# Hourglass attention and a gated MLP on one core: a replanned start and q, k loads in three pieces

## Chip, core and metric

The kernel runs on one core of one Trainium2 chip. Its engines are TensorE (PE), ScalarE (ACT), VectorE (DVE), GpSimd (POOL) and SyncE (SP, which only issues DMAs here). The metric is the device time of one execution in microseconds (us), the median of several.

## What is computed

q, k, v have the shape 8 x 8 x 576 x 64 (batch, head, position, value). The attention has two parts that are added: one over means of four neighbouring positions (144 of them), spread back over the four, and a local one in which each position sees only those less than four away.

```python
q_d = q.reshape(B, H, Sd, factor, D).mean(axis=3)      # k_d, v_d alike
out_d = sm_attn(q_d, k_d, v_d)
out_up = np.repeat(out_d, factor, axis=2)
mask = np.abs(pos[:, None] - pos[None, :]) < factor
scores = np.where(mask, scale * np.matmul(q, k.transpose(0, 1, 3, 2)), -1000000000.0)
out_local = np.matmul(softmax(scores), v)
attn = out_up + out_local                              # -> x, 4608 x 512
h = x @ w_in                                           # 512 x 2048
g = h * (1.0 / (1.0 + np.exp(-h)))
return g @ w_out                                       # 2048 x 512
```

## The kernel before

**Work.** The 64 heads are handled as 32 pairs of heads; pairs 4b to 4b+3 are batch b, and batch b gives 576 of the 4608 rows of x. For each pair p the jobs are:

- loads of q and k (into tile qkb as bf16, cast by the DMA that POOL issues; pair 0 comes in float32 into qk and is cast by DVE and ACT) and of v (four jobs lv p h j on SP, 64 x 5 rows of 64 values each, cast by POOL in job cv);
- T: 36 transposes of 64 x 64 on PE (line 810), then the evictions eq and ek from PSUM into qT and kT (line 565), and two sums over four positions on DVE (line 845);
- S: scores (20 + 4 + 8 matmuls with the mask's bias for the first eight pairs), then two exponentials on ACT (line 893);
- Z: sums of the exponentials (12 matmuls), on DVE turned into factors (lines 964, 968, 974);
- VP: means of v (9 matmuls) for the first eight pairs, evicted as vd;
- PV: 28 matmuls, then m on DVE (line 990) and a on POOL (line 1018), which writes the pair's part of xT.

G1 is x times w_in, 9 blocks of 512 rows with 16 groups of 4 matmuls each; a group is followed by a tanh on ACT (line 1043) and a product on DVE (line 1047). G2 is the product with w_out, 4 x 4 parts of 4 matmuls per block. The first block of G1 needs batch 0 only, the second needs batches 0 and 1. All matmuls but the transposes are recorded under line 571, the helper mm.

**Order.** Nothing of the order is written out. The class Plan simulates the jobs in Python while the kernel is built: each job has costs, jobs that it waits for, buffers and PSUM banks that it takes, and a due time; each engine, when it comes free, takes the ready job with the smallest due time. The order that results on each engine is what the program holds, so each engine and each issuing queue runs strictly in that order. For PE the function pick prefers jobs of kind A (those of pairs 0 to 7), then visits V of later pairs, then G1 and G2. D(p, left) gives the due times: 22 + 1.5 (p - 3) - left for pairs 0 to 3, and 42 + 3 (p - 7) - left for pairs 4 to 7. For T left is 8.5, for S 6.5, for Z 4.5, for VP 4.0 and for PV 2.4.

Four things in Plan.run matter here:

- PE jobs that start before COLD[0] us are taken to last COLD[1] times as long.
- Before WARM_END, when the planner sees PE idle ahead of a job, it puts filler matmuls in front of it (jb.fill): products of the constant tile dz into a free PSUM bank, whose results nobody reads.
- code and FETCH stand for the loading of PE's instructions: a job with mm matmuls takes 2 mm instructions, and after each 256 of them PE waits until FETCH us after the last such wait (5.2 before 110 us, then 4.5). But the constructor of Job sets mm to 0 after it has taken the keywords, so that no job has a count and the model is never used.
- The weights are issued by POOL as w0 to w7 (four pieces of w_in, four of w_out), each behind a gate, W_GATE: w0 after pair 2's last v load has landed, w1 to w4 after that of pairs 4 to 7, w5 to w7 after the issue of k of pairs 8 to 10. load_order holds back the loads of pairs 4 to 7 in the plan until pair 3's last v load is issued, and those of pair 8 until w2 has landed.

```python
n = int((now - max(busy["PE"], self.freed[b]) - WARM_GAP) / 0.43 if now < WARM_COLD else
        (now - max(busy["PE"], self.freed[b]) - WARM_GAP) * WARM_PART / 0.22)
if n > 0:
    j.fill = (n, b)
```

The planner reaches each engine's queue: what it moves on PE moves with its evictions on ACT and DVE, its a jobs on POOL and its loads on POOL and SP.

Of the kernel before, what the change touches and what calls it, by code (L numbers as in the profile page):

```python
# [6 lines left out]
AF = mybir.ActivationFunctionType  # L7
# [3 lines left out]
BF16 = mybir.dt.bfloat16  # L11
# [5 lines left out]
NPAIR = B_ * H_ // 2  # L17
NSUP = 9
XR = 2048
COLD = (8.0, 1.65)  # L20
WARM_END, WARM_GAP, WARM_PART, WARM_COLD = 115.0, 0.4, 0.6, 7.0
FETCH = (5.2, 110.0, 4.5)
ALONE = 0.8
TW = 8
N_QK, N_VS, N_VQ, N_QKB, N_VB, N_VD, N_T, N_P, N_ZR, N_RB, N_XO = 1, 4, 2, 6, 5, 5, 3, 4, 2, 2, 3
GS_PE = 0
VP_PE = 8

SPLIT = 8
# [5 lines left out]
LEAD = 6  # L35
K_ENG = "DVE"
FRESH = 2.2


CV_ENG = "POOL"  # L40
# [10 lines left out]


def E_ENG(p, x):
    return ("ACT", "DVE") if p < 8 else "ACT"


def G_ENG(p, x):
    return ("DVE", "ACT")


def G1_BANKS(j):
# [26 lines left out]
def HOLD(p):  # L88
    return ["S3"] if p == 4 else []
# [148 lines left out]
class Job:  # L238
# [3 lines left out]
    def __init__(self, name, eng, cost, emit, **kw):  # L242
        self.name, self.emit = name, emit
        self.eng = (eng,) if isinstance(eng, str) else eng
        self.cost = cost if isinstance(cost, dict) else {e: cost for e in self.eng}
        self.pre, self.take, self.use, self.bank, self.marks = (), (), (), None, {}
        self.due, self.work, self.port, self.kind, self.thr, self.gran = 0.0, 0.0, False, None, None, 0.093
        for k, v in kw.items():
            setattr(self, k, v)
        self.ran, self.last, self.succ, self.end, self.mm, self.fill = None, None, [], None, 0, None  # L250


class Plan:
# [241 lines left out]
def bass_hourglass_attn__then__act_silu_kernel(  # L495
# [9 lines left out]
    with kctx:  # L505
# [25 lines left out]
        vs = sb("vs", [128, 10, 64], F32, N_VS)  # L531
        vq = sb("vq", [128, 4, 256], F32, N_VQ)
        vt = sb("vt", [128, 4, 128], F32)
        qkb = sb("qkb", [128, 2, 576], BF16, N_QKB)
        vb = sb("vb", [128, 10, 64], BF16, N_VB)
        vd = sb("vd", [128, 4, 64], BF16, N_VD)
        qT = sb("qT", [128, S_], BF16, N_T)
# [133 lines left out]
        def rows(t, p, n, off):  # L671
            return bass.AP(tensor=t.tensor, offset=t.offset + (128 * p + off) * 576, ap=[[576, n], [1, 576]])

        def dma(name, eng, out_, in_, r, w, sem, work, cost, hold=(), **kw):
            def emit(j):
                P.op(j.ran, lambda s: s.dma_start(out_(), in_()), r() if r else [], w(), sem(), after=gates(hold))  # L676
            kw["pre"] = list(kw.get("pre", ())) + list(hold)
            J(name, eng, cost, emit, work=work, **kw)

        def loads(p, order):  # L680
            if p == 0:
                dma("lkx", LD_ENG("kx", 0), lambda: kx[64:128, :], lambda: rows(k, 0, 64, 0), None, lambda: rkx, lambda: "kx",
                    0.45, 0.43, due=order["kx"], take=[("qkb", -1)])
            for x, (t, n, off) in enumerate(((q, 128, 0), (k, 128 if p < NPAIR - 1 else 64, 64))):
                if p in SW:
                    dma(f"c{'qk'[x]}{p}", "POOL", lambda x=x, n=n: qkb[S("qkb", p)][0:n, x, :],
                        lambda t=t, n=n, off=off: rows(t, p, n, off), None, lambda x=x: [R(f"qkb{S('qkb', p)}{x}")],
                        lambda x=x: f"qkb{S('qkb', p)}{x}", 0.87, 0.57, gran=0.106, take=[("qkb", p)], due=-60 + p if p < 4 else D(p, 26.0),
                        hold=order.get(("gate", p), ()))
                    continue  # L690
                dma(f"l{'qk'[x]}{p}", LD_ENG("qk"[x], p), lambda x=x, n=n: qk[S("qk", p)][0:n, x, :],
                    lambda t=t, n=n, off=off: rows(t, p, n, off), None, lambda x=x: [R(f"qk{S('qk', p)}{x}")],
                    lambda x=x: f"qk{S('qk', p)}{x}", 0.85 * n / 128, 0.43, take=[("qk", p)] + ([("qkb", 0)] if p == 0 else []), due=order["qk", p],
                    hold=order.get(("gate", p), ()))
            for h in range(2):
                for j in range(2):
                    def emit(jb, h=h, j=j):
                        s = S("vs", p)
                        sem, w = f"vs{s}{h}{j}", [R(f"vs{s}{h}{j}")]
                        base = v[(2 * p + h) // H_, (2 * p + h) % H_]  # L700
                        T_, o = base.tensor, base.offset + (288 * j - 3) * D_
                        d, lo, hi = vs[s][half(j), 5 * h:5 * h + 5, :], 0, 5
                        if (p, h, j) == (0, 0, 0):
                            lo = 1
                            P.op(jb.ran, lambda e: e.dma_start(vs[s][3:64, 0, :], bass.AP(
                                tensor=T_, offset=base.offset, ap=[[64, 61], [1, 64]])), [], w, sem, after=gates(["vz"] + list(order.get(("gate", p), ()))))
                        if (p, h, j) == (NPAIR - 1, 1, 1):
                            hi = 4
                            P.op(jb.ran, lambda e: e.dma_start(vs[s][64:123, 9, :], bass.AP(
                                tensor=T_, offset=base.offset + 517 * D_, ap=[[64, 59], [1, 64]])), [], w, sem)  # L710
                        P.op(jb.ran, lambda e: e.dma_start(d[:, lo:hi, :], bass.AP(
                            tensor=T_, offset=o + 58 * 64 * lo, ap=[[64, 64], [58 * 64, hi - lo], [1, 64]])), [], w, sem,
                            after=gates(order.get(("gate", p), ())))
                    J(f"lv{p}{h}{j}", LD_ENG("v", p), 0.64, emit, work=0.39, gran=0.018, take=[("vs", p)],
                      due=order["v", p], pre=list(order.get(("gate", p), ())) + (["vz"] if p == 0 else []))
            if p >= VP_PE:
                def emit(jb):
                    i = S("vq", p)
                    base = v[2 * p // H_, 2 * p % H_]
                    T_, o = base.tensor, base.offset  # L720
                    P.op("SP", lambda e: e.dma_start(vq[i][:, 0:4:2, :], bass.AP(
                        tensor=T_, offset=o, ap=[[256, 128], [S_ * D_, 2], [1, 256]])), [], [R(f"vqm{i}")], f"vq{i}")
                    for j in range(2):
                        P.op("SP", lambda e, j=j: e.dma_start(vq[i][64 * j:64 * j + 16, 1:4:2, :], bass.AP(
                            tensor=T_, offset=o + 128 * 256, ap=[[256, 16], [S_ * D_, 2], [1, 256]])),
                            [R(f"vqc{i}1"), R(f"vqc{i}3")], [R(f"vqe{i}{j}")], f"vqe{i}{j}")
                J(f"lvq{p}", "SP", 1.6, emit, work=0.85, gran=0.046, take=[("vq", p)], due=order["vq", p],
                  pre=list(order.get(("gate", p), ())) + [f"vqz{(p - VP_PE) % N_VQ}"])
# [18 lines left out]
        def casts(p):  # L747
# [2 lines left out]

            def one(x):
                def emit(jb):
                    P.op(jb.ran, lambda e, a=i(), b=j(): copy(jb.ran, e, qkb[b][:, x, :], qk[a][:, x, :]),
                         [R(f"qk{i()}{x}")], [R(f"qkb{j()}{x}")])
                return emit

            if p == 0:
                def emit(jb):
                    P.op("ACT", lambda e, b=S("qkb", -1): e.activation(qkb[b][64:128, 1, :], kx[64:128, :], AF.Copy),
                         rkx, [R(f"qkb{S('qkb', -1)}1")])  # L760
                J("ckx", "ACT", 0.65, emit, pre=["lkx"], take=[("qkb", -1)], due=D(0, 9.4))
            use = dict(take=[("qkb", p)], use=[("qk", p)])
            if p in SW:
                pass
            elif p < CAST2:
                for x in range(2):
                    eng = C_ENG[p][x]
                    J(f"c{'qk'[x]}{p}", eng, {"DVE": 0.5, "ACT": 0.65, "POOL": 0.6}, one(x), pre=[f"l{'qk'[x]}{p}"],
                      port=True, due=D(p, 9.3), **use)
            else:  # L770
                def emit(jb):
                    P.op("POOL", lambda e, a=i(), b=j(): e.tensor_copy(qkb[b][:, :, :], qk[a][:, :, :]),
                         [R(f"qk{i()}0"), R(f"qk{i()}1")], [R(f"qkb{j()}0"), R(f"qkb{j()}1")])
                J(f"cq{p}", "POOL", 1.15, emit, pre=[f"lq{p}", f"lk{p}"] + HOLD(p), port=True, due=D(p, 10.3), marks={f"ck{p}": 1.0}, **use)

            def emitv(jb):
                a, b = S("vs", p), S("vb", p)
# [24 lines left out]
        def pe_T(p):  # L802
            a, b = S("qkb", p), S("qkb", p - 1)
            tiles = ((0, 0, 0, a), (0, 1, 1, a), (1, 1, 0, a), (1, 0, 1, b))
            for r in range(9):
                for j, h, x, n in tiles:
                    t, c = t_home(p, x, r)
                    o = PS[half(h), t, c:c + 32].bitcast(BF16)
                    w = qkb[n][half(j), x, 64 * r:64 * r + 64]
                    P.op("PE", lambda e, o=o, w=w, j=j: e.transpose(o, w, idn[half(j), :]),  # L810
                         [R("idn"), R(f"qkb{n}{x}")], [rB[t]])

# [6 lines left out]

        def after_T(p):  # L820
            keys = dict(take=[("T", p)])
            grp = p < GS_PE

            def evict(x):
                def emit(jb):
# [471 lines left out]
```

## Time and profile before

| | us |
|---|---|
| median of 3 runs | 341.86 (341.33 to 343.66) |
| the profiled execution | 342.31 |
| its span, first to last instruction | 340.5 |
| PE busy in the span | 326.8 |
| mean clock granted to TensorE | 0.970 of full |
| first matmul of G1 | 36.32 after the span's start |
| first matmul of G2 | 73.05 |

All times inside the profile count from the span's start. A busy share of PE is not a share of its peak: matmuls overlap in the array, and their ends are modelled. In a row of the timeline the bracket at the end gives the idle time of the engine before it and what ended it; "issue" there means that nothing the profile shows was waited for. A DMA share is the mean over the core's 16 DMA engines; it can pass 1. Queue 0 holds the DMAs that POOL issues, queue 1 those of SP, queue 10 those of ACT, queue 8 code.

### The profile page before, as it was taken

What the parts mean: (1) busy time and instruction counts of PE and PEld (TensorE: products, weight loads), DVE (VectorE), ACT (ScalarE), POOL (GpSimd) and SP (SyncE); (2) the same over time, 40 slices, a digit from 0 to 9 for tenths busy, and PEclk for the clock granted to TensorE, in tenths of its full rate; (3) what the DMA queues carried; (4) which work ended last, traced back from release to release, by engine and by line L of the source; (5) the groups of instructions that cost most, each with busy time, mean ns of one, the idle gap of its engine ahead of it and who ended that gap; (6) DMA issues with size and microseconds to landing.
All of it is one profiled execution on the core that took longest, in us unless ns stands there. A gap on an engine that the chain in (4) does not pass through costs nothing.

```text
span 340.5 us, 10780 instructions
## 1 busy us (share of the span) xinstructions
PE 326.8 (96%) x4623; PEld 213.9 (63%) x4623; DVE 229.6 (67%) x410; ACT 179.0 (53%) x317; POOL 156.6 (46%) x211
## 2 busy tenths in 40 slices
PE   5587999999999999999999999999999999999996
PEld 2465677865555775587557755785577558866544
DVE  6586989866667885788577857796767556754200
ACT  5542756665544765476447645664656416644221
POOL 7363498435679667970698068704400140000000
PEclk9755999999999999999999999999999999999999
DMA  8997879999878976996398339500100010000112
GB/s 168 175 252 156 255 181 212 198 229 234 172 178 195 213 177 151 209 202 174 76 240 180 81 57 249 115 1 33 66 31 2 33 64 31 2 1 31 62 64 92
DMA packets 70666, 44.59 MB, mean 131 GB/s; under 512 B 45914, under 2 KB 63770, under 8 KB 70618
## 3 DMA queue, kind: packets, MB, share of 16 engines
q1 hardware_dynamic: 56378, 28.00, 30.8%
q0 software_dynamic: 13088, 15.36, 26.2%
q8 instruction: 36, 0.59, 0.7%
q10 hardware_dynamic: 1152, 0.54, 0.7%
q14 instruction: 12, 0.10, 0.1%
HBM read 45.61 MB, written 9.44 MB: 162 GB/s over the span
## 4 chain that ended last, share of the span: by engine, by line
PE 92%; DMA 2%; DVE 2%; issue 2%; POOL 1%; ACT 0%; POOLq 0%
PE PS L571 89%; PE PS L810 3%; DMA qkb<-in_k_dram 2%; DVE Pt L899 1%; POOL qkb L676 0%; DVE qd L845 0%; POOL gT L601 0%; DVE Rb L974 0%; DVE qT L565 0%; DVE kd L845 0%; DVE zt L964 0%; DVE zr L968 0%; ACT osb L1076 0%; DVE vd L565 0%; POOL idw L610 0%
## 5 line engine op out<-in xcount | busy, mean ns | idle before, releaser
L571 PE MATMUL PS<-xT,w_in_sb 128*128 128x512 f32 x576 | 141.2, 399 | 0.0
L571 PE MATMUL PS<-w_out_bf,gT 128*128 128x512 bf16 (+1 forms) x592 | 131.3, 374 | 0.0
L571 PEld LDWEIGHTS PS<-xT,w_in_sb 128*128 128x128 f32 x576 | 106.7, 188 | 24.7 <-DVE gT L1047 0.7
L1047 DVE SCALAR_TENSOR_TENSOR gT<-th,PS 128x512 bf16<-128x512 f32 x144 | 96.9, 683 | 37.0 <-ACT th L1043 36.3
L1043 ACT ACTIVATE th<-PS 128x512 f32<-128x512 f32 x144 | 86.1, 599 | 54.2 <-PE PS L571 46.0
L571 PEld LDWEIGHTS PS<-w_out_bf,gT 128*128 128x128 bf16 x592 | 54.7, 98 | 62.9 <-issue 3.5
L1018 POOL TENSOR_TENSOR xT<-xo 128x576 fp32r<-128x576 f32 (+5 forms) x48 | 43.5, 919 | 51.5 <-DVE xo L990 51.4
L565 POOL CAST vb<-vs 128x640 bf16<-128x640 f32 x32 | 24.4, 767 | 57.3 <-PE PS L571 42.5
L1100 ACT ACTIVATE osb<-PS 128x512 f32<-128x512 f32 x35 | 21.1, 603 | 53.6 <-PE PS L571 53.6
L893 ACT ACTIVATE Pt<-PS 128x576 bf16<-128x576 f32 x32 | 20.8, 649 | 33.0 <-PE PS L571 32.8
L785 POOL TENSOR_TENSOR vt<-vq 128x512 f32<-128x512 f32 x24 | 30.8, 1285 | 10.0 <-DMA vq<-in_v_dram 9.9
L990 DVE TENSOR_TENSOR xo<-PS,Rb 128x720 f32<-128x720 f32 x32 | 28.6, 893 | 5.1 <-PE PS L571 4.9
L974 DVE STREAM_TRANSPOSE Rb<-zr 128x768 f32<-128x768 f32 x32 | 30.9, 964 | 0.1
L899 DVE TENSOR_TENSOR Pt<-Pt,mask 128x576 bf16<-128x576 bf16 x24 | 16.3, 677 | 20.9 <-ACT Pt L893 20.9
L565 ACT ACTIVATE qT<-PS 128x576 bf16<-128x576 bf16 x30 | 19.8, 659 | 9.4 <-PE PS L810 9.4
L810 PE MATMUL PS<-idn,qkb 64*64 64x64 bf16 x1152 | 17.5, 201 | 7.5 <-issue 3.9
L845 DVE TENSOR_REDUCE qd<-qT 128x144 bf16<-128x576 bf16 x32 | 22.9, 716 | 1.5 <-ACT qT L565 1.4
L845 DVE TENSOR_REDUCE kd<-kT 128x144 bf16<-128x576 bf16 x32 | 23.0, 718 | 0.0
L964 DVE STREAM_TRANSPOSE zt<-PS 128x96 f32<-128x96 f32 x32 | 8.8, 274 | 20.2 <-PE PS L571 20.2
L565 ACT ACTIVATE kT<-PS 128x576 bf16<-128x576 bf16 x30 | 20.0, 665 | 1.6 <-PE PS L810 1.6
L810 PEld LDWEIGHTS PS<-idn,qkb 64*64 64x64 bf16 x1152 | 14.2, 115 | 9.5 <-issue 4.5
L676 POOL DMA_DIRECT2D qkb<-in_k_dram x31 | 17.1, 553 | 5.1 <-PE PS L810 5.1
(56 smaller groups left out, 229.3 us busy)
## 6 DMA issues: line engine op xcount, KB each, us to landing
vs<-in_v_dram SPq DMA_DIRECT2D x123, 80.0 KB, 4.6
out_dram<-osb SPq DMA_DIRECT2D x35, 256.0 KB, 3.6
vq<-in_v_dram SPq DMA_DIRECT2D x24, 256.0 KB, 4.3
qkb<-in_q_dram POOLq DMA_DIRECT2D x31, 144.0 KB, 5.0
qkb<-in_k_dram POOLq DMA_DIRECT2D x30, 144.0 KB, 5.4
w_in_sb<-in_moe_w_in_dram POOLq DMA_DIRECT2D x4, 1024.0 KB, 7.4
w_out_bf<-in_moe_w_out_dram POOLq DMA_DIRECT2D x4, 512.0 KB, 14.3
vq<-in_v_dram SPq DMA_DIRECT2D x48, 32.0 KB, 3.9
```

The lines of the kernel that those rows point to most:

```text
L565: return e.activation(out_, in_, AF.Copy) if eng == "ACT" else e.tensor_copy(out_, in_)
L571: P.op("PE", lambda t: t.matmul(out_, lhsT, rhs, start=start, stop=stop, skip_group_check=True), r, w)
L785: P.op("POOL", lambda g: g.tensor_tensor(vt[:, :, :], vq[n][:, :, 0:128], vq[n][:, :, 128:256], ALU.add), [R(f"vqm{n}"), R(f"vqe{n}0"), R( ...
L810: P.op("PE", lambda e, o=o, w=w, j=j: e.transpose(o, w, idn[half(j), :]), [R("idn"), R(f"qkb{n}{x}")], [rB[t]])
L845: P.op("DVE", lambda e: e.tensor_reduce(dst, src.rearrange("p (g r) -> p g r", r=4), AX.X, ALU.add), [R(f"{'qk'[x]}T{s}")], [R(f"{'qk'[x]} ...
L893: P.op("ACT", lambda e: e.activation(d[:, :, :], PS[:, b[0]:b[1] + 1, a:e_], AF.Exp, scale=sc), [rB[b[0]], rB[b[1]]], [R(f"P{m}" if local ...
L974: P.op("DVE", lambda e: e.transpose(Rb[n][:, :].rearrange("p (c q) -> p c q", q=32), zr[z][:, :].unsqueeze(2).to_broadcast([128, 24, 32])) ...
L990: P.op("DVE", lambda e: e.tensor_tensor(xo[x][:, :, :], PS[:, bb[0]:bb[1] + 1, 0:360], Rb[u][:, :].rearrange("p (x c) -> p x c", x=2)[:, : ...
L1018: P.op("POOL", lambda g, dst=dst, in0=in0, in1=in1: g.tensor_tensor(dst, in0, in1, ALU.add), [R(f"xo{x}")], xblk(kc, t + a, t + e_))
L1043: P.op("ACT", lambda e: e.activation(th[x][:, :], PS[:, b, :], AF.Tanh, scale=0.5), [rB[b]], [R(f"th{x}")])
L1047: P.op("DVE", lambda e: e.scalar_tensor_tensor(gT[j % 2][:, f, :], th[x][:, :], 1.0, PS[:, b, :], ALU.add, ALU.mult), [rB[b], R(f"th{x}")] ...
L1100: P.op("ACT", lambda e, s=S("osb", n), b=bank(key)[0]: e.activation(osb[s][:, :], PS[:, b, :], AF.Copy, scale=0.5), [rB[bank(key)[0]]], [R ...
```

## The change

Every edit is in the start of the kernel or in the planner:

- the model of code loading comes into use, since mm is no longer reset; PE jobs count 1.5 times their cost until 34 us of the plan, not 1.65 times until 8 us;
- WARM_END is 0, so no fillers are put in (the memset of dz stays);
- the evictions of T of pairs 5 to 7 may go to ACT only, those of pairs 0 to 4 to ACT or DVE as before;
- a row of q or k (576 values) is loaded in three pieces of 192, each to its own 200-value stretch of qkb; the transposes and the casts of pair 0 follow that layout;
- a branch in casts that no pair took is left out, and GS_PE and G_ENG are written in another form with the same effect here.

By the planner's new costs, jobs of pairs 0 to 3 come ahead of those of pairs 4 to 7 where both are ready.

```diff
-COLD = (8.0, 1.65)
-WARM_END, WARM_GAP, WARM_PART, WARM_COLD = 115.0, 0.4, 0.6, 7.0
+COLD = (34.0, 1.5)
+WARM_END, WARM_GAP, WARM_PART, WARM_COLD = 0.0, 0.4, 0.6, 7.0
...
-GS_PE = 0
+GS_PE = ()
...
+AD = ("ACT", "DVE")
+E_EARLY = (AD, AD, AD, AD, AD, "ACT", "ACT", "ACT")
...
 def E_ENG(p, x):
-    return ("ACT", "DVE") if p < 8 else "ACT"
+    return E_EARLY[p] if p < 8 else "ACT"
...
+        self.mm = 0
         for k, v in kw.items():
             setattr(self, k, v)
-        self.ran, self.last, self.succ, self.end, self.mm, self.fill = None, None, [], None, 0, None
+        self.ran, self.last, self.succ, self.end, self.fill = None, None, [], None, None
...
-        qkb = sb("qkb", [128, 2, 576], BF16, N_QKB)
+        qkb = sb("qkb", [128, 2, 3, 200], BF16, N_QKB)
...
+        def rows_3(t, p, n, off):
+            return bass.AP(tensor=t.tensor, offset=t.offset + (128 * p + off) * 576, ap=[[576, n], [192, 3], [1, 192]])
+
+        def parts(x):
+            return x.rearrange("p (a b) -> p a b", a=3)
...
-                    dma(f"c{'qk'[x]}{p}", "POOL", lambda x=x, n=n: qkb[S("qkb", p)][0:n, x, :],
-                        lambda t=t, n=n, off=off: rows(t, p, n, off), None, lambda x=x: [R(f"qkb{S('qkb', p)}{x}")],
+                    dma(f"c{'qk'[x]}{p}", "POOL", lambda x=x, n=n: qkb[S("qkb", p)][0:n, x, :, 0:192],
+                        lambda t=t, n=n, off=off: rows_3(t, p, n, off), None, lambda x=x: [R(f"qkb{S('qkb', p)}{x}")],
...
-                    w = qkb[n][half(j), x, 64 * r:64 * r + 64]
+                    w = qkb[n][half(j), x, r // 3, 64 * (r % 3):64 * (r % 3) + 64]
...
-            grp = p < GS_PE
+            grp = p in GS_PE
```

More of the change, by code (lines that the diff above doesn't have):

```diff
@@ L37 @@
 FRESH = 2.2
+AD = ("ACT", "DVE")
+E_EARLY = (AD, AD, AD, AD, AD, "ACT", "ACT", "ACT")
+G_EVICT = ("DVE", "ACT")
 CV_ENG = "POOL"
@@ L53, in E_ENG @@
 def E_ENG(p, x):
-    return ("ACT", "DVE") if p < 8 else "ACT"
+    return E_EARLY[p] if p < 8 else "ACT"
 def G_ENG(p, x):
-    return ("DVE", "ACT")
+    return G_EVICT
 def G1_BANKS(j):
@@ L752, in emit @@
                 def emit(jb):
-                    P.op(jb.ran, lambda e, a=i(), b=j(): copy(jb.ran, e, qkb[b][:, x, :], qk[a][:, x, :]),
+                    P.op(jb.ran, lambda e, a=i(), b=j(): copy(jb.ran, e, qkb[b][:, x, :, 0:192], parts(qk[a][:, x, :])),
                          [R(f"qk{i()}{x}")], [R(f"qkb{j()}{x}")])
@@ L758, in emit @@
                 def emit(jb):
-                    P.op("ACT", lambda e, b=S("qkb", -1): e.activation(qkb[b][64:128, 1, :], kx[64:128, :], AF.Copy),
+                    P.op("ACT", lambda e, b=S("qkb", -1): e.activation(qkb[b][64:128, 1, :, 0:192], parts(kx[64:128, :]), AF.Copy),
                          rkx, [R(f"qkb{S('qkb', -1)}1")])
@@ L769, in casts @@
                       port=True, due=D(p, 9.3), **use)
[L770 to L774, printed above, removed]
             def emitv(jb):
```

## The prediction

> **What bounds the kernel now.** I read the page first, then busy time by stretch, then TensorE's timeline of the first 45 us, then the times at which loads landed.
>
> From the page: each engine's busy share, the slices, the queues.
>
> ```profile
> PE 326.8 (96%) x4623; PEld 213.9 (63%) x4623; DVE 229.6 (67%) x410; ACT 179.0 (53%) x317; POOL 156.6 (46%) x211
> ...
> PE   5587999999999999999999999999999999999996
> ...
> PEclk9755999999999999999999999999999999999999
> ...
> q1 hardware_dynamic: 56378, 28.00, 30.8%
> q0 software_dynamic: 13088, 15.36, 26.2%
> q8 instruction: 36, 0.59, 0.7%
> ```
>
> PE is full from the fifth slice on. What can be won lies in the first 36 us, where the clock is also half. The 36 packets of queue 8 load code: 0.59 MB in 36 pieces is 16 KB each, and 4623 matmuls and as many weight loads over 36 are 257, so one piece holds about 256 of PE's instructions, that is 128 matmuls.
>
> Busy time by stretch (first two columns: stretch and length; then busy time, with counts, of PE, PEld, DVE, ACT, POOL; granted clock; DMA share; GB/s):
>
> ```profile
> 12.00:16.00 4.00, 2.56 (x104) 1.83 (x93) 1.41 (x2) 3.15 (x6) 2.06 (x4) 0.69 0.86 159
> 20.00:24.00 4.00, 2.88 (x95) 2.33 (x90) 3.86 (x9) 1.55 (x4) 2.83 (x4) 0.50 1.20 314
> 24.00:28.00 4.00, 2.48 (x67) 1.78 (x64) 1.69 (x3) 0.72 (x3) 0.90 (x1) 0.50 1.22 213
> 28.00:32.00 4.00, 3.60 (x83) 2.35 (x82) 2.54 (x5) 1.58 (x3) 1.51 (x2) 0.50 0.73 159
> 32.00:36.00 4.00, 4.00 (x132) 2.30 (x132) 4.00 (x9) 2.27 (x4) 2.40 (x3) 0.63 0.38 86
> 36.00:40.00 4.00, 4.00 (x100) 3.07 (x92) 4.00 (x8) 3.16 (x7) 1.67 (x3) 1.00 1.01 278
> ```
>
> The clock is 0.50 to 32 us and 1.00 from 36. The clock's own records put the rise at 34.93, after 17.07 us at half. PE is not idle after 28.4.
>
> PE's timeline (start, length, what, count, idle time before it and its releaser):
>
> ```profile
> 16.56 0.22 PE L810 MATMUL PS<-idn,qkb 64*64 64x64 bf16 x4 [2.00 <-issue]
> ...
> 21.94 0.27 PE L571 MATMUL PS<-qT,kT 64*64 64x58 bf16 x5 [1.12 <-issue]
> ...
> 28.40 0.43 PE L810 MATMUL PS<-idn,qkb 64*64 64x64 bf16 x16 [1.92 <-issue]
> ...
> 29.35 0.61 PE L571 MATMUL PS<-dz 128*128 128x512 bf16 x1
> ...
> 31.32 0.47 PE L571 MATMUL PS<-Pt,vb 64*64 64x58 bf16 x20
> ...
> 33.90 1.31 PE L571 MATMUL PS<-dz 128*128 128x512 bf16 x3
> ...
> 36.32 2.11 PE L571 MATMUL PS<-xT,w_in_sb 128*128 128x512 f32 x8
> ```
>
> The three waits on nothing ("issue", 5.04 us) fall 128 matmuls apart: they are waits for code. PE ran out again 5.38 and 6.46 us after it resumed, whatever it had to do. So to 28.4 us PE is paced by code, and fillers (dz) and early transposes of pairs 4 and 5 spend that code. The product with w_in (G1) begins at 36.32; pair 3's PV, the last it needs, began at 31.32.
>
> **The change part by part.** Times are against the profiled execution: 342.31 us, a span of 340.5 and 1.8 around it. That is 0.45 above the median, 341.86.
>
> *Fillers gone.* There are 23. The six from 29.35 on stand in a stretch without idle time. From each row's start to the next: 0.40 (29.35 to 29.75), 0.54, 0.54, and 1.24 for the three at 33.90, in all 2.72 us. Freed time at half clock is worth half, and the clock rises when it rises: up to 33.90 the work slides by 1.48; the 1.18 us from 35.14 to 36.32 at full clock then take 2.36 at half from 32.42 and end at 34.8. So G1 could follow at 34.8, not 36.32: **-1.5**. Ends: 0 and -2.7. The 13 fillers from 1.46 on and those at 9.7 ran while PE waited for q and k: removing them frees nothing there.
>
> *Code spent on fillers.* 17 fillers ran before 28.4: 34 of 256 instructions, at 5.9 us a piece (mean of 5.38 and 6.46): **-0.8**, ends 0 and -0.9.
>
> *Batch 0 first.* The planner now keeps the matmul counts that it used to reset to 0, so it sees code waits, and it takes 1.5 times as long for PE jobs until 34 us. Batch-0 jobs have the earlier due times, so when PE comes out late it finds them ready and takes them. T4 (at 22.19) and T5 (26.00 to 28.8), 72 matmuls, move behind PV3; so do T6, S4. A pair has 117 matmuls (36, 32, 12, 9, 28 for T, S, Z, VP, PV); four are 936 instructions, below the boundary at 960. PV3 then ends near 25 to 26 instead of 32.05, and with m3 and a3 behind it (2.75 us from PV3's end to a3's end at 34.80 now) G1 can start near 28.5; w0 landed at 25.75. But PE has no idle time after 28.4 now, so G1 in front of T4 to T7 only swaps work: **0** by itself. The cover: batch 1's chain on DVE and ACT must end before the second block of G1 (below). On POOL a3 comes earlier, and w1 (issued 34.75, behind a3) can come as early as its gate, the landing of pair 4's v at 29.75. SP's order of v loads keeps its due times.
>
> *Clock.* The rise followed a stretch, 31.5 to 34.9, without idle time; the one before it began 0.3 us before PE resumed at 28.40 and did not raise it. If PE is busy without a break about 1.8 us earlier, the rise comes about as much earlier on average, and half of that is won: **-0.9**. Ends: +1.7 (a stretch of 3.41 us later, at half clock: the fillers were what kept it busy) and -1.7 (one earlier). The Trainium skill, "TensorE: Matmul & The Clock Gate" (What's actually happening), has the clock released after a busy window of some 3.4 us that is free-running; by that rule alone G1 itself would release it, and this term would be -1.7 or 0. The trace's stretches of 3.41 us agree.
>
> *q and k in three pieces.* A row of 1152 bytes in SBUF becomes three packets of 384. In the trace's packet records a 1152-byte packet took 106 ns (median), a 256-byte one of v 18, a 1024-byte one of vq 46. A piece costs between 18 and 46 by size, or 106/3 = 35 by share; I take 42, since a row with the cast cost more than an uncast one of 2304 bytes (93): 126 against 106, +19%, or 0.16 us on each of 16 engines for a load (8 rows each). While both queues had work (18 to 26 us) about as many v packets as q,k or weight packets passed, so q,k lose ground to v. v of pair 0 landed at 13.8 and of pair 4 at 26.9 to 29.8: these come earlier, and q,k of pairs 1 to 3 (8.21 to 13.23) later. T1 and T2 wait for k now (1.5 us in all), and T0 to T2 run at half clock (0.69 against 0.48 for 36 transposes): **+0.5**, ends -0.5 and +2.5 (shares from 85 to 64%). The Trainium skill, "DMA: Bandwidth & Descriptors" (Specifications), says that under 512 B a transfer is read, modified and written; if that doubles a piece, see the third rival. The 256-byte packets here show no such step.
>
> *Code through the same engines.* The fetch of a piece of code started 2.5, 3.0 and 4.2 us after PE resumed while the DMA share was above 1, and 1.2 after it at a share of 0.4. Turns of 42 ns in place of 106 shorten that. I take 0.4 us for each of three pieces: **-1.2**. Ends +1.5 (three times the packets stand ahead) and -3.2.
>
> *POOL's issues.* An issue of 128 packets takes 553 ns, of 512 (weights) 780; 384 give 704, +0.15. With two loads each of seven pairs that is 2.1 us on a POOL that was idle 3.6 us before 27.10 and 2.1 before 30.45: **0**; without that cover a0 to a3 slide by up to 1.2. In all 61 loads add 9 us to POOL's 156.6.
>
> *Evictions of pairs 5 to 7 on ScalarE.* Of the six only qT of pair 7 (36.66, 0.70 us) was on DVE: **0**, ends +0.3 and -0.3; it trades 0.70 of DVE for 0.65 of ACT.
>
> Sum: -1.5 - 0.8 + 0 - 0.9 + 0.5 - 1.2 = -3.9, so 338.4 for a profiled execution and **338.0** on the median (-1.1%).
>
> **The rivals.**
>
> *Batch 1 comes late (slower).* From T7 (35.91) to PV7 (56.60) it took 20.7 us, and the second block of G1 starts at 57.51. DVE had for each pair 0.72 + 0.72 + 0.27 + 0.29 + 0.96 + 0.89 = 3.85 us and for four G1 groups 2.73: 26.3 for four pairs, 29 at the 91% it is filled from 36 to 56. Begun at 28 it ends at 57, with a7 (1.2) at 58.2: then nothing is won. If pair 7's T7 also falls behind the first G1 groups, to 41, and takes 20.7 again, PE has run out of G1 and G2 (w_out lands to 71.14) and waits 5 us at about 57: 347 at worst, **345.5** typically (the waits for code still won). It decides where T7 passes about 37. For it: DVE at 4.00 of 4 from 32 to 40. Against: DVE idles 2.3 of 4 us at 24 to 28.
>
> *The gains cancel.* q,k come 2 us later, code waits stay, no earlier clock: -1.5 - 0.8 + 2.0 = -0.3: **341.5**. For it: PE waited for k of pairs 1 and 2.
>
> *Small packets cost double.* 84 ns a piece, 252 a row: eight pairs' 16 loads take 16 x 8 x 146 ns = 18.7 us more of each engine, some of it hidden in the 0.73 and 0.38 of 28 to 36; half left is +9, less 2.3: **348.5**.
>
> **How the numbers follow.** About 1%, 3.4 us, is what a measurement of this kernel can tell from no change. Forecast 0.60 (its own range 334 to 340.5; over 1% faster 0.50, within 0.10), cancelling 0.15 (within), batch 1 late 0.20 (slower), packets double 0.05 (slower). So 0.50 faster, 0.25 same, 0.25 slower. The range is 334.0 to 345.5: the low end takes fillers -2.7, code -3.2 and the clock -1.7 with landing +0.5 (-7.9); the high end is the late batch, and the worse half of it and the double packets are left out.
>
> **What would show it.** Right: no dz rows; PV of pair 3 before 28 us; G1 before 33; "issue" waits under 4 us in all before 30; clock 1.00 by 35; v of pair 0 landed before 11; no PE wait near 57. Wrong: PE idle between 36 and 60 waiting for w_in_sb, gT or xT; POOL issues well over 0.70 us; G1 still after 35.

## The result and the profile after

The changed kernel took **347.32 us** (346.32 to 348.18, 4 runs) against 342.15 for the kernel before on the same chip (4 runs). The ratio is 1.0165, 95% interval 1.0139 to 1.0191: slower by 1.65%. The prediction was 338.0 with a range of 334.0 to 345.5, so it had the sign wrong and the time lies outside its range. Medians here and below are over all executions; ratios and intervals leave out seven that ran in a slower state (two of e1, three of e12, one each of e9 and e13). The profiled execution of the changed kernel took 346.32.

From the page of the changed kernel, the same rows as before:

```profile
PE 322.0 (93%) x4600; PEld 212.6 (62%) x4600; DVE 228.0 (66%) x410; ACT 179.0 (52%) x317; POOL 169.7 (49%) x211
...
PE   1586996999999999999999999999999999999996
...
PEclk9995998999999999999999999999999999999999
...
q1 hardware_dynamic: 56378, 28.00, 31.6%
q0 software_dynamic: 28832, 15.36, 31.6%
...
q8 instruction: 36, 0.59, 0.7%
```

There are two dips now. The first is the start, as before. The second is the seventh slice, 51.7 to 60.3 us, where the kernel before was full: PE drops to 6 tenths. Queue 0 has 28832 packets for the same 15.36 MB and takes 31.6% of the engines' time, not 26.2.

PE's timeline of the changed kernel shows the waits for code, the end of batch 0, the first G1, and the second dip:

```profile
17.23 0.45 PE L575 MATMUL PS<-mbias,nidn 64*64 64x288 bf16 x3 [0.57 <-issue]
...
23.70 0.28 PE L575 MATMUL PS<-Pd,hot 128*64 128x96 bf16 x5 [1.38 <-issue]
...
27.24 0.47 PE L575 MATMUL PS<-Pt,vb 64*64 64x58 bf16 x20
...
30.21 0.59 PE L816 MATMUL PS<-idn,qkb 64*64 64x64 bf16 x28 [1.92 <-issue]
31.64 0.84 PE L816 MATMUL PS<-idn,qkb 64*64 64x64 bf16 x36 [0.83 <-ACT qT L569]
32.41 2.07 PE L575 MATMUL PS<-xT,w_in_sb 128*128 128x512 f32 x4
...
42.86 0.45 PE L816 MATMUL PS<-idn,qkb 64*64 64x64 bf16 x33 [0.27 <-issue]
...
53.01 0.40 PE L575 MATMUL PS<-Pd,vd 64*64 64x72 bf16 x8
56.52 4.56 PE L575 MATMUL PS<-xT,w_in_sb 128*128 128x512 f32 x12 [3.11 <-issue]
61.01 0.35 PE L575 MATMUL PS<-Pt,vb 64*64 64x58 bf16 x20
```

Batch 0 does come first: PV of pair 3 begins at 27.24 (31.32 before) and G1 at 32.41 (36.32 before). Then PE stands for 3.11 us in front of G1 matmuls whose data are there (batch 0's part of xT was complete at 31.22, the last piece of w_in landed at 43.86), and the next 12 of them take 4.49 us from start to start, where 12 take 2.7 at full clock (the 68 in a row from 57.51 in the kernel before took 15.5).

Busy time by stretch, the changed kernel:

```profile
48.00:52.00 4.00, 4.00 (x76) 3.15 (x69) 3.05 (x6) 2.90 (x6) 3.98 (x6) 1.00 1.22 179
52.00:56.00 4.00, 1.41 (x67) 0.89 (x65) 3.67 (x8) 1.69 (x3) 4.00 (x6) 1.00 1.32 190
56.00:60.00 4.00, 3.48 (x9) 2.77 (x9) 0.69 (x1) 0.60 (x1) 3.00 (x4) 0.57 1.20 230
```

The same stretches in the kernel before, and from its timeline the row of the 68 matmuls:

```profile
48.00:52.00 4.00, 4.00 (x39) 3.07 (x38) 3.24 (x7) 1.79 (x4) 4.00 (x7) 1.00 1.22 274
52.00:56.00 4.00, 4.00 (x50) 2.79 (x49) 3.87 (x8) 2.31 (x5) 3.29 (x5) 1.00 1.22 197
56.00:60.00 4.00, 4.00 (x78) 3.05 (x77) 3.67 (x7) 2.65 (x5) 3.51 (x6) 1.00 1.19 229
...
57.51 15.70 PE L571 MATMUL PS<-xT,w_in_sb 128*128 128x512 f32 x68
```

In the changed kernel the wait also cost the clock: it is 0.57 in the stretch behind it (the clock's records have half clock from 56.44 for 3.41 us).

A mark that stands in every version is the 65th matmul of G1, the start of its second block. It is at 59.4 us in the kernel before and at 64.4 in the changed one; from there to the end it takes 281.0 and 280.1. So the loss lies before that mark, and nearly all of it after 36 us. The kernel before goes from 36.32 to the mark in 23.1 us without idle time. The changed one takes 28.2 us from 36.14; without its waits (0.32 for a copy on ACT, 0.27 and 3.11 for code) and without the 1.7 us by which half clock lengthened the 12 matmuls it would be 22.8. So at 36 us it was only some 0.5 us ahead, fillers gone and all, and then it lost 5.4. The four microseconds won at the start of G1 were worth nothing by then: the same work of pairs 4 to 7 was still to be done.

### The profile page after: what moved, and what is told of

It is laid out like the page before. It is cut to its first block, busy times and chain, and to the rows that moved or that the text cites. A ratio compares the mean times of both kernels' runs of the same rounds, so it can differ in the third digit from the quotient of the medians.

```text
span 344.5 us, 10723 instructions
## 1 busy us (share of the span) xinstructions
PE 322.0 (93%) x4600; PEld 212.6 (62%) x4600; DVE 228.0 (66%) x410; ACT 179.0 (52%) x317; POOL 169.7 (49%) x211
## 3 DMA queue, kind: packets, MB, share of 16 engines
q1 hardware_dynamic: 56378, 28.00, 31.6%
q0 software_dynamic: 28832, 15.36, 31.6%
## 4 chain that ended last, share of the span: by engine, by line
PE 92%; DMA 3%; issue 2%; POOL 2%; DVE 1%; ACT 1%; POOLq 0%
PE PS L575 88%; PE PS L816 3%; DMA qkb<-in_k_dram 3%; POOL qkb L686 1%; POOL gT L605 0%; DVE Rb L980 0%; DVE xo L996 0%; ACT qT L569 0%; ACT th L1049 0%; ACT osb L1082 0%; ACT vd L569 0%; DVE zr L974 0%; DVE zt L970 0%; POOL idw L614 0%; POOL cv L605 0%
## 5 line engine op out<-in xcount | busy, mean ns | idle before, releaser
L575 PE MATMUL PS<-xT,w_in_sb 128*128 128x512 f32 x576 | 150.3, 410 | 3.1 <-issue 3.1
L575 PE MATMUL PS<-w_out_bf,gT 128*128 128x512 bf16 (+1 forms) x592 | 133.6, 374 | 0.0
L575 PEld LDWEIGHTS PS<-xT,w_in_sb 128*128 128x128 f32 x576 | 108.7, 191 | 29.1 <-issue 3.2
L575 PEld LDWEIGHTS PS<-w_out_bf,gT 128*128 128x128 bf16 x592 | 53.6, 98 | 63.6 <-issue 6.9
L569 POOL CAST vb<-vs 128x640 bf16<-128x640 f32 x32 | 23.5, 737 | 47.3 <-PE PS L575 41.3
L816 PE MATMUL PS<-idn,qkb 64*64 64x64 bf16 x1152 | 18.3, 203 | 14.4 <-DVE qkb L569 7.4
L686 POOL DMA_DIRECT2D qkb<-in_k_dram x31 | 23.9, 770 | 12.1 <-PE PS L816 12.1
L569 ACT ACTIVATE qT<-PS 128x576 bf16<-128x576 bf16 x31 | 20.5, 661 | 10.9 <-PE PS L816 10.9
L905 DVE TENSOR_TENSOR Pt<-Pt,mask 128x576 bf16<-128x576 bf16 x24 | 14.3, 597 | 15.9 <-ACT Pt L899 15.9
L686 POOL DMA_DIRECT2D qkb<-in_q_dram x31 | 24.3, 784 | 0.0
## 6 DMA issues: line engine op xcount, KB each, us to landing
w_out_bf<-in_moe_w_out_dram POOLq DMA_DIRECT2D x4, 512.0 KB, 13.8
```

Of the source, the lines that this page charges most:

```text
L569: return e.activation(out_, in_, AF.Copy) if eng == "ACT" else e.tensor_copy(out_, in_)
L575: P.op("PE", lambda t: t.matmul(out_, lhsT, rhs, start=start, stop=stop, skip_group_check=True), r, w)
```

## The experiments

The first theory after the result was **code**: with batch 0 first, the short matmuls of pairs 4 to 7 come between 36 and 53 us, 128 of them every 5 us, while the loads keep the DMA engines full and code arrives late. In the trace's packet records the piece of code that PE waited for at 53 us was fetched 6.1 us after PE had passed the boundary before it (48.1 to 54.15; the boundaries lie 128 matmuls apart); at 40 to 45 us it took 2.8 and 2.9. Its packet ended at 55.13 and PE went on 1.4 us later; after the three pieces that PE waited for in the kernel before, this took 1.3 to 1.4. The rival was **pieces**: three times the packets, which delay loads and code everywhere, with any order. A third was that the **fillers** had kept the clock up. "Before" below is always the kernel before, run on the same chip.

### e1 to e3: one part each

e1 takes only the new loads (the layout of qkb, rows_3 and parts, as in the change). e2 takes them out of the changed kernel. e3 leaves the fillers out of the kernel before:

```diff
-            if jb.fill:
+            if False:
                 for _ in range(jb.fill[0]):
```

> The kernel before with q and k rows in three pieces of 192 and nothing else; the order on every engine is that of before. Theory code (the new order puts too many of PE's short instructions into 37 to 53 us, where code arrives late): here the code waits before 30 us grow by at most 1 us, no wait near 53, time within 1 us of before. Theory pieces (three times the packets delay code and q, k everywhere): 345 to 347, with a code wait of 2 us or more between 40 and 60 us. The 0.77 us that an issue on POOL takes in the changed kernel is expected in both.

> The changed kernel with whole rows of 576 values loaded, all else and the order kept. Theory code: still slower than before, 344 to 347, with the wait for code near 53 us at 2 us or more and a half-clock stretch behind it. Theory pieces: back to 342 or below, no wait for code near 53.

> The kernel before with its 23 fillers left out of PE's stream and the planned order kept. My term for them (-1.5 for those after 28.4 us and -0.8 for their code): 339.5 to 340. Rival, that the fillers keep the clock: the rise to full clock comes one stretch of 3.41 us later or the early jobs lose as much as the fillers cost, 342 to 344.

| | us | ratio to before | 95% interval | second block of G1 |
|---|---|---|---|---|
| e1, pieces only | 344.94 | 1.0094 | 1.0064 to 1.0124 | 61.9 |
| e2, all but the pieces | 343.45 | 1.0061 | 1.0030 to 1.0093 | 60.5 |
| e3, no fillers only | 342.55 | 1.0030 | 1.0000 to 1.0059 | 60.3 |

Neither theory had it alone. The pieces cost 0.94% in the old order and the order 0.61% with whole rows; together that is 1.55, near the 1.65 measured. e1 was below the 345 to 347 of the theory pieces and had no wait near 53; e2 was faster than the theory code said, and showed its wait, shorter than expected and without half clock behind it.

PE's timeline of e1, rows with idle time:

```profile
12.40 0.69 PE L810 MATMUL PS<-idn,qkb 64*64 64x64 bf16 x35 [0.72 <-DMA qkb<-in_k_dram]
17.77 0.27 PE L810 MATMUL PS<-idn,qkb 64*64 64x64 bf16 x4 [2.11 <-issue]
24.52 0.27 PE L571 MATMUL PS<-qT,kT 64*64 64x58 bf16 x5 [1.67 <-issue]
30.97 0.43 PE L810 MATMUL PS<-idn,qkb 64*64 64x64 bf16 x16 [1.92 <-issue]
```

The same three rows in the kernel before stand at 16.56, 21.94 and 28.40. T2's k lands 1.0 us later (12.40 against 11.38), the next two pieces of code come 1.2 and 2.6 us later, and G1 starts at 38.8. The clock's records have the rise at 37.04, not 34.93.

PE's timeline of e2:

```profile
15.88 0.45 PE L575 MATMUL PS<-mbias,nidn 64*64 64x288 bf16 x3 [1.80 <-issue]
...
54.14 3.06 PE L575 MATMUL PS<-xT,w_in_sb 128*128 128x512 f32 x12 [1.59 <-issue]
```

With whole rows the wait at the same place is 1.59 us, and 12 matmuls take 3.06: no half clock behind it. So the wait of 3.1 let the clock fall, this one of 1.6 did not (more on this in the last section). The piece of code came 4.4 us after the boundary here, 6.1 with pieces.

PE's timeline of e3:

```profile
28.48 0.47 PE L571 MATMUL PS<-Pt,vb 64*64 64x58 bf16 x19 [2.16 <-issue]
32.62 0.39 PE L571 MATMUL PS<-qd,kd 64*64 64x144 bf16 x8 [0.19 <-DVE kd L845]
33.86 0.45 PE L571 MATMUL PS<-Pt,hot 128*64 128x96 bf16 x6 [0.85 <-ACT Pt L893]
```

Without the fillers PE resumed at 28.48, as late as with them, but further on: it had 476 matmuls of real work behind it, not 459, since no code went into 17 fillers. Where the later fillers had stood, PE now waits for DVE and ACT (1.04 us in these two rows), and the clock's records have the rise at 38.49, one stretch of 3.41 us and a little later than with fillers. The rival that I had named for e3 came out, in its range of 342 to 344.

### e4 to e6: the other parts alone

e4 is the evictions alone, e5 the kept counts alone (the constructor of Job as in the change), e6 keeps the fillers before 12 us only:

```diff
-    return ("ACT", "DVE") if p < 8 else "ACT"
+    return ("ACT", "DVE") if p < 5 else "ACT"
...
-            if jb.fill:
+            if jb.fill and jb.start < 12.0:
```

> The kernel before with the evictions of pairs 5 to 7 on ScalarE only, planned anew with that. My term 0: 341 to 342.5. Rival, that ScalarE becomes late for the tanh of G1 or the last pairs of batch 1: 343.5 or more, with a PE wait on ACT between 33 and 57 us.

> The kernel before with the planner keeping the counts of matmuls, so that it models the loading of code; fillers, the old cold factor, evictions and whole rows as before. If the order that the model makes is by itself what costs (batch 0 first, short instructions crowded behind the start of G1): 343 to 345 with a wait for code between 45 and 56 us. If the crowding comes only with the 34 us of cold factor and the evictions: 341 to 342 and no such wait.

> The kernel before with its first 16 fillers (before 12 us) kept and the seven later ones left out, order kept. If the later fillers only stand in the way, as my term said: 339.5 to 340.5, G1 at 35. If they keep the clock: the rise comes at 38.3 rather than 34.9 and the time is 341.5 to 343.

e4: 341.18, ratio 0.9983 (0.9950 to 1.0016). e5: 341.89, 1.0010 (0.9976 to 1.0044). e6: 342.35, 1.0012 (0.9978 to 1.0045). None differs from before; e4 came out as I expected, and of my two cases for e5 the one without crowding. My term for the late fillers, -1.5 us, is refuted by e6: the interval's lower end is -0.8. In its trace the clock rises at 37.49, where I had named 38.3 for the case that the late fillers keep it. The kept counts alone make no crowded order.

### e7: is the wait at 53 us really for code?

e7 is the changed kernel with the same order in which the transposes of pairs 4 to 7 are 20 wide ones per pair, not 36 (128 instructions fewer):

```diff
+WIDE = (4, 5, 6, 7)
...
+            if p in WIDE:
+                for r in range(0, 9, 2):
...
+                                o = PS[half(h), t, c:c + 64].bitcast(BF16)
+                                w, i_ = qkb[a][:, x, r // 3, 64 * (r % 3):64 * (r % 3) + 64], idw[:, :]
```

> The changed kernel, its order kept, with the transposes of pairs 4 to 7 as 20 wide ones in place of 36 per pair, which puts wrong values into qT and kT of those pairs but the same amount of data: 128 of PE's instructions fewer before 53 us, PE's time about the same. Theory code (the wait near 53 us is for the next 256 instructions): the wait of 3.1 us and the half-clock stretch behind it go, 343 to 345. Theory that batch 1's chain or something else holds PE there: PE still waits 3 us near 53, 346.5 to 348.

e7: 344.40, ratio 1.0076 (1.0045 to 1.0107), 2.9 us below the changed kernel's median and in the range of the theory code. Its timeline at the place where PE had stood:

```profile
55.60 0.40 PE L576 MATMUL PS<-Pd,vd 64*64 64x72 bf16 x8
55.93 3.01 PE L576 MATMUL PS<-xT,w_in_sb 128*128 128x512 f32 x12
```

The matmuls follow without idle time and at full clock. The data that G1 reads are no earlier than in the changed kernel (batch 0's part of xT is complete at 31.57, the last piece of w_in is issued at 34.37, not 34.02), only PE has fewer instructions to fetch: the wait was for code. The wide transposes save no time on PE itself: 16 of them took 0.64 us at full clock (at 40.46), 36 narrow ones 0.48 in the changed kernel (at 38.03). From there to the mark PE has no idle row either, so pair 7's chain was in time. The profiled execution was the slowest of the ten (346.55), so its later part is no measure of the gain.

### e8 and e9: where the pieces cost

e8 loads pairs 1 to 7 in pieces and the rest whole, e9 the other way round (there split_ returns p >= 8), in the order of before:

```diff
+        def split_(p):
+            return 0 < p < 8
...
+        def place(a, p):
+            return a.rearrange("p (a b) -> p a b", a=3)[:, :, 0:192] if split_(p) else a[:, 0:576]
```

> The kernel before with three pieces for pairs 1 to 7 only, whole rows from pair 8 on, order kept. If the pieces cost through the start (k of pair 2 lands 1 us later, each code wait before 31 us is longer, full clock 2 us later): as e1, 344 to 345.5. If they cost through the load on the DMA engines and POOL all along: 341.5 to 342.5.

> The kernel before with three pieces from pair 8 on only, order kept. If the pieces cost through the start: 341 to 342.3. If they cost all along: 343.5 to 345.

e8: 343.93, ratio 1.0071 (1.0048 to 1.0093). e9: 342.16, 1.0032 (1.0002 to 1.0061). About two thirds of the pieces' cost comes through the start (e8's three code waits end at 17.04, 24.07 and 31.35, its second block is at 62.1), and a third from pair 8 on, which is barely clear of no change. e9's profile (second block at 59.0) shows no place for the later third, and cannot: that execution took 341.42, no longer than the median of before beside it (341.39). That part stays unexplained.

### e10 to e14: what the order costs without the wait, and what helps

e10 is e2 with e7's wide transposes; e11 has the kept counts and the evictions together, with fillers and whole rows; e12 is e2 with 16 fillers put back ahead of T of pairs 0 and 2; e13 and e14 repeat e10 and e4 with more runs.

> The changed kernel's order with whole rows and with the transposes of pairs 4 to 7 as 20 wide ones (wrong values in qT and kT of those pairs). If the new order costs only through the wait for code near 53 us (1.6 us in e2): 341.2 to 342.3, no such wait, about e3's time less up to 1 us. If it costs through something else: 343 to 344 as e2.

> The kernel before with the planner's counts kept and the evictions of pairs 5 to 7 on ScalarE, planned anew; fillers, whole rows and the old cold factor stay. Each alone gave no difference: together 340.5 to 342.5 if nothing crowds; 343 or more, with a wait for code between 45 and 56 us, if the two together make the crowded order.

> The changed kernel with whole rows and with 16 fillers put back ahead of T of pairs 0 and 2, where PE waits for loads anyway; order kept. If the missing early fillers are part of what e2 lost (clock at half from the start): 341.5 to 342.7, below e13's or e2's 343.4. If they are not: 343 to 344 as e2.

> The same kernel as e10 (changed order, whole rows, wide transposes of pairs 4 to 7 with wrong values), since five runs left it between 0.3 and 1.1% above before. If the order costs only through the code wait near 53 us: 341.2 to 342.7. If it costs by itself: 343 to 344, with no PE wait above 1 us after 36 us to show for it, but a later second block of G1.

> The same kernel as e4 (before, evictions of pairs 5 to 7 on ScalarE). If it is a better kernel than before: 340.3 to 341.3 and an interval below 1. If not: within 0.3% of before.

| | us | ratio to before | 95% interval |
|---|---|---|---|
| e10, order, whole rows, wide transposes | 343.09 | 1.0069 | 1.0032 to 1.0107 |
| e11, counts and evictions | 344.03 | 1.0084 | 1.0065 to 1.0103 |
| e12, order, whole rows, early fillers | 343.32 | 1.0045 | 1.0020 to 1.0070 |
| e13, as e10 | 342.11 | 1.0031 | 1.0004 to 1.0059 |
| e14, as e4 | 341.11 | 1.0004 | 0.9983 to 1.0024 |

e10 (five runs) fell where I expected a cost beyond the code wait, 343 to 344; e13, the same kernel with twelve, fell where I expected the wait alone to cost, at +0.31%, about as much as the missing fillers alone (e3, +0.30%). By e13 the order itself costs nothing once the code wait is gone; e10's interval, 0.32 to 1.07%, lies above that, so this is likely, not shown. Neither shows a gain. The intervals of e2 and e13 overlap, so that the wait costs the difference (0.3%) with whole rows is likely, not shown; with pieces e7 shows it. e12 still waits 1.12 us at 53.84 and lies between; its time is the one that I expected if the early fillers are no part of the loss (343 to 344). e11 fell into another order: neither part alone changed the time, together they cost 0.84%, and in its trace the second block of G1 starts at 61.9, behind 64 matmuls (T of pair 9, S of pair 8) that come later in the other versions, with no code wait after 36 us; I did not find its cause. No version here beats the kernel before.

## Why the prediction was wrong

*Fillers gone, -1.5.* Wrong. Taking out those after 12 us changed nothing (e6, +0.12%), taking out all cost 0.3% (e3, interval from 0 to 0.6). I took the stretch after 28.4 us as full of work because it had no idle time; what the fillers filled were in part waits for DVE and ACT, and the clock's rise moved from 34.9 to 37.5 and 38.5 (in two executions of one kernel, e4 and e14, it was at 32.4 and 33.5, so about 1 us of that can be chance). My end of 0 for this term, and the clock term's end of +1.7, were the right ones.

*Code spent on fillers, -0.8.* The code was saved: at 28.4 us e3 is 17 matmuls further on. But the time was lost again to the waits for DVE and ACT and to the later rise of the clock, and e3 took longer, not less. (The 5.38 and 6.46 us run from one resumption of PE to the next; in between it worked for 4.26 and 4.54.)

*Batch 0 first, 0.* Right that it happens and that an earlier G1 is worth nothing by itself (likely, by e13). Wrong in the cover that I named: I asked whether batch 1's chain on DVE and ACT would end in time, and did not ask whether PE's own code would. I had counted instructions against code in the start, and not again for pairs 4 to 7. Between 36 and 53.5 us PE now had 363 short matmuls and 36 of G1, where it had 231 and 48 before: three pieces of code in place of two, at a DMA share of 1.14 in place of 0.92, and the one that PE ran out of came 6 us after the boundary. This is the step that failed: I called the swap of work worth 0, and a new wait for code at 53 us, 3.11 us with half clock behind it, came with it, 0.89 of the 1.65% (e7). Most of the signs that I had named for being right came all the same: no dz rows, PV of pair 3 at 27.24, G1 at 32.41, waits for code of 3.87 us in all to 30.21. They were signs of the start, and the loss came after it.

*Clock, -0.9.* Not borne out: in the changed kernel it rose at 35.96, 1.0 us later than before (no more than e4 and e14 differ), then fell again for 3.41 us after the code wait, a stretch that no term of mine had.

*Pieces, +0.5.* The mechanism was right (v of pair 0 landed at 11.96, not 13.8; k of pair 3 at 14.94, not 13.23), the size was off: a piece took 51 ns in the median, not 42, so a row takes 153 and not 126; alone the pieces cost 3.4 us (e1), beyond my end of +2.5. By size this term failed as much as the wait for code, and the two overlap: with whole rows the wait was 1.59 us, with pieces 3.11.

*Code through the same engines, -1.2.* Wrong sign. In e1 each of the two pieces of code behind the first was fetched 4.2 us after PE resumed; before, 3.0 and 4.2. Shorter turns did not bring the code earlier; the piece at 53 us came after 6.1 us with pieces and 4.4 without. The "Three times the packets stand ahead" end of this term (+1.5) was nearer.

*POOL's issues, 0.* They took 0.77 us each where I said 0.70. That they cost nothing is not shown: k of pair 3 was issued at 6.08, not 4.86, and in every run the pieces and their longer issues come together. *Evictions, 0.* Right alone (e4, e14), not beside the kept counts (e11).

*The rivals.* "Batch 1 comes late" named the place (PE idle near 57 before the second block) and the sign, but the cause was another: PE's code, not pair 7's chain. (The 57.51 that I took for the start of the second block is the start of the first block's last two groups; the second starts at 59.4.) "Small packets cost double" was nearer than I gave it chance for: 153 ns for 106 is half as much again. The page of the Trainium skill that I named there, "DMA: Bandwidth & Descriptors" (Specifications: under 512 B a transfer is read, modified and written), pointed to the right side, though these rows show no doubling.

## What to carry to other kernels

Count a program's instructions against its code loading wherever short ones are moved, not only where the waits for code stand today: find the spacing from the rows that wait on nothing ("issue"), and lay it over the new order together with the DMA share of that stretch. Idle time that fillers occupy is not free time: before taking them out, look for what the engine would wait on in their place, and for the clock. Cutting loads into smaller packets let another queue through here (v of pair 0 landed 1.8 us earlier), and it cost engine time, 153 ns a row for 106; the code that PE waited for near 53 us came later too, 6.1 us after its boundary and not 4.4.

## What was not expected of the hardware

A wait of 3.1 us on TensorE was followed by 3.41 us at half clock; waits of 1.6 (e2) and 1.1 us (e12) near 53 us were not. But in the start shorter ones were: 2.00 us in the kernel before (half clock from 17.86), 1.38 in the changed one (from 25.72). The length of one wait does not decide. From its first record on, the clock of each run goes by stretches of 3.41 us, and a fall goes with PE's idle time inside one stretch. In the 16 profiles the clock fell 20 times, each time after a stretch with 1.38 us or more of idle time, to 3.03 us; of the stretches with more than 1.38 us only seven, of 1.40 to 1.70 us, did not bring a fall. The 3.11 us of the changed kernel lay almost whole in one stretch (3.03 us of it in 53.03 to 56.44), the 1.59 us of e2 in two (0.45 and 1.14). The clock rose 20 times, each time after a stretch with at most 0.37 us of idle time; ten more such stretches at half clock brought no rise, so this is not the whole condition. It fits the fillers: the stretch before the rise in the kernel before, 31.52 to 34.93, had no idle time, and in e6 the one from 30.67 to 34.08 had 1.16 us and brought no rise.

The length of the stretch agrees with the Trainium skill, "TensorE: Matmul & The Clock Gate" (What's actually happening), which puts the window of the clock at about 3.4 us. Its table there has the clock fall after a window that is idle; here 1.4 to 3.0 us of idle time in a window were followed by the fall.

A copy with its 576 output values in three stretches of 192 took 0.74 us on VectorE, and 0.45 in one stretch (the cast of pair 0, float32 to bf16). On ScalarE both took 0.68.

The clock column of a page tells nothing before the clock's first record: in the changed kernel it reads 1.00 up to 22 us, while 35 transposes took 0.69 us there, the time that they have at half clock in the kernel before.
